# A gated MLP's products computed turned, and a short product placed inside a longer one, in an attention and two-MoE kernel

## The chip, the cores and the metric

The kernel runs on one core of one Trainium2 chip. A core has five engines with a queue each: TensorE (PE, matrix products; PEld is its weight load), VectorE (DVE), ScalarE (ACT), GpSimd (POOL) and SyncE (SP, which issues most DMAs). The metric is the device time of one execution in microseconds (us): the median of three runs of the kernel before is 655.77 us (653.97 to 659.06).

## The reference

Three layers follow one another on 1152 tokens (two sequences of 576) of width 512. In the attention each query keeps its 32 largest scores:

```python
scores = scale * np.matmul(q, k.transpose(0, 1, 3, 2))        # 2 x 8 heads, 576 x 576, head width 64
kth = np.partition(scores, -top_k, axis=-1)[..., -top_k:-top_k + 1]
scores = np.where(scores >= kth, scores, -1000000000.0)
...
x = x / rms * rms_g                                           # first MoE: a gated MLP
g = xn @ w_gate                                               # 512 x 1536
silu = g * (1.0 / (1.0 + np.exp(-g)))
x = silu * (xn @ w_val) @ w_out                               # 1536 x 512
...
expert_idx = np.argmax(x @ w_gate2, axis=1)                   # second MoE: 8 experts, one per token
out[i] = gate_w[i] * (relu(x[i] @ w1[e]) @ w2[e])             # 512 -> 1024 -> 512
```

## The kernel before

**Tiles and stages.** The tokens go in nine tiles t of 128. The attention goes in 36 pairs p of heads, four to a tile: scores (PE, L317; copied by ACT, L319), the search for the 32nd largest value (DVE, L324 to L379), weights (ACT L398 and L404, POOL L399), transposes (PE L422) and products with the values (PE L430). When the four pairs of a tile are done, `norm(t)` makes `xn`, the normed tile with features on the partitions (last step: ACT L470, DVE L471), `moe1(t)` computes the first MoE, and `dispatch(t)` sends the tile's rows into the DRAM buffer `disp`, sorted by expert (POOL L621). Then come the experts of the second MoE, e = 0 to 7, each with an up product, a down product and a send of rows to the output.

**The first MoE (L479 to L536).** Every f32 matrix is kept as a high and a low f16 half, and one product takes three f16 matmuls (high by high, high by low, low by high). A tile has six blocks b of 512 hidden features, a gate block and a value block for each of three groups g. One block is 12 matmuls at L502: a 128x128 piece of `xn` is loaded, 512 columns of weight stream through, and the result `a` has tokens on the partitions. Gate and value are joined elementwise into `h` (L509 to L523). Before the down product, `turned` (L483) transposes `h` with four f32 matmuls (L486) into a PSUM tile, and `halves` (L469) makes `hT` from it on ACT (L470) and DVE (L471). The down product is 36 matmuls a tile (L531). In the last tile, t = 8, `after(...)` fixes which PE instruction follows which.

**What sets the order.** Each stage is a generator. A table of slots says which generator steps when (`at`, L693 to L713), `ahead` gives a step a priority, and a scheduler with a clock of its own places every instruction into its engine's queue from these priorities and from what is free. Each engine then works through its queue in order, and an instruction that waits holds all behind it. So an edit that changes the number and the length of matmuls can move other work in every queue.

**The tail.** While tiles 7 and 8 finish, the first expert weights are loaded as f32 (L779; tiles `raw` and `split`), squared on ACT to find a scale (`size`, L795), and split into f16 halves by ACT (L820) and DVE (L822, L825). `dispatch(7)` and `dispatch(8)` follow the last two tiles: on DVE `scr` (L606) gives each token its place, POOL's L621 scatters the rows. Expert 0's rows come in two parts: `gather("a", ...)` (SP, L836) fetches the 128 rows that tiles 0 to 7 have surely filled ("a"), and `rest_gather` (POOL L903, SP L907) fetches 48 later rows into `xbT` ("b"). `gather(1, ...)` fetches expert 1's rows. On PE the order of the source is `up("a")`, `down("a")`, `up("b")`, `send("a")`, `up(1)`, all products at L920.

## Time and profile before

| quantity | kernel before |
|---|---|
| median of 3 runs | 655.77 us (653.97 to 659.06) |
| profiled execution | 654.35 us, of which span 652.4 us |
| PE busy | 583.8 us (89%), 4817 matmuls |
| PE weight loads busy | 409.2 us (63%) |
| DVE busy | 533.5 us (82%) |
| ACT busy | 501.6 us (77%) |
| POOL busy | 355.6 us (55%) |

The span is the time between the first and the last instruction of the trace; the profiled execution's own time is 1.95 us more. Matmuls overlap, so the busy time of PE is not a sum of work: the distance from one matmul's start to the next one's, which a row with a count gives, is what a matmul takes from the engine. In a row, `x12` counts instructions, and `[2.98 <-DMA xbT<-xb]` says that the engine stood idle for 2.98 us before the row and which event ended that.

### The profile page before, as it was taken

Reading aid. Unit: us, or ns where it says so; the run is one execution under the profiler, and the core shown is the slowest. Engines: PE = TensorE matmul, PEld = TensorE weight load, DVE = VectorE, ACT = ScalarE, POOL = GpSimd, SP = SyncE. Lnnn points to the kernel's source line nnn. Section 1 sums busy time; section 2 is a strip of 40 time slices with the busy share of each in tenths; the row PEclk is TensorE's granted clock in tenths of the full one; section 3 lists DMA queues with packets and bytes.
Section 4 is the critical chain, followed back from the end, with each engine's and each line's share of the span. In section 5 each row is a group of like instructions: output and inputs, shape, how many; then the busy total and the mean of one; then the engine's idle time right before and its main releaser. Section 6 shows DMA issues by size and latency. Waiting matters only on the chain.

```text
span 652.4 us, 13434 instructions
## 1 busy us (share of the span) xinstructions
PE 583.8 (89%) x4817; PEld 409.2 (63%) x4817; DVE 533.5 (82%) x1439; ACT 501.6 (77%) x972; POOL 355.6 (55%) x490
## 2 busy tenths in 40 slices
PE   1427879799999999999999999999999879999995
PEld 1314455445666666767666666565555579999994
DVE  3989999968989979998988999882359756999951
ACT  4469978997787968978887889786499538999811
POOL 2487644646358879958878789686121310123312
PEclk9999979899999999999999999999999989999998
DMA  8998345923000010100000000004900479999201
GB/s 233 296 329 292 118 175 194 311 76 78 30 13 29 14 49 10 34 18 26 18 10 34 16 13 14 2 1 179 354 16 8 156 192 390 340 321 359 97 23 43
DMA packets 47006, 80.05 MB, mean 123 GB/s; under 512 B 18716, under 2 KB 23324, under 8 KB 46930
## 3 DMA queue, kind: packets, MB, share of 16 engines
q1 hardware_dynamic: 45138, 74.28, 35.2%
q0 software_dynamic: 1792, 4.83, 1.9%
q8 instruction: 39, 0.64, 0.4%
q14 instruction: 37, 0.30, 0.1%
HBM read 64.35 MB, written 12.27 MB: 117 GB/s over the span
## 4 chain that ended last, share of the span: by engine, by line
PE 61%; DMA 10%; DVE 9%; ACT 8%; POOL 6%; issue 3%; SPq 2%; POOLq 0%; DVEq 0%; ACTq 0%
PE pm L502 16%; PE acc L920 15%; PE pm L531 9%; PE xps L430 6%; PE tp L317 5%; PE tp L422 4%; ACT junk L795 3%; DMA disp<-wraw 2%; DMA wbig<-in_k_l_dram 2%; DVE r L373 2%; PE pm L486 2%; POOL pp L399 1%; DVE wbig L168 1%; DMA raw<-in_w_dram 1%; DVE wbig L169 1%
## 5 line engine op out<-in xcount | busy, mean ns | idle before, releaser
L502 PE MATMUL pm<-wbig,xn 128*128 128x512 f16 x600 | 145.4, 379 | 0.5 <-DVE hT L471 0.5
L920 PEld LDWEIGHTS <-split 128*128 128x128 f16 x1728 | 114.8, 99 | 5.1 <-DMA xbT<-xb 3.2
L399 POOL TENSOR_TENSOR pp<-s,pp 128x576 f32<-128x576 f32 x72 | 102.1, 1434 | 23.1 <-ACT pp L398 22.9
L502 PEld LDWEIGHTS <-xn 128*128 128x128 f16 x648 | 62.6, 98 | 60.6 <-issue 0.9
L376 DVE MAX8 m<-r 128x8 f32<-128x288 f32 x216 | 96.7, 452 | 2.5
L373 DVE MATCH_REPLACE8 r<-m,r 128x288 f32<-128x288 f32 x216 | 95.2, 443 | 0.0
L317 PE MATMUL tp<-kst,qh 128*128 128x288 f32 (+1 forms) x160 | 64.4, 410 | 32.8 <-ACT s L319 14.9
L531 PE MATMUL pm<-wbig,hT 128*128 128x512 f16 x324 | 76.7, 380 | 0.0
L825 DVE SCALAR_TENSOR_TENSOR split<-raw,sc,split 128x2048 f16<-128x2048 f32 (+1 forms) x32 | 65.9, 2076 | 0.1
L319 ACT ACTIVATE s<-tp 128x288 f32<-128x288 f32 x144 | 57.3, 421 | 10.5 <-PE tp L317 8.8
L423 ACT ACTIVATE pt<-tp 128x384 f32<-128x384 f32 x108 | 52.2, 503 | 15.3 <-PE tp L422 10.8
L317 PEld LDWEIGHTS tp<-kst,qh 128*128 128x128 f32 (+1 forms) x160 | 31.1, 195 | 51.1 <-ACT s L319 21.1
L430 PE MATMUL xps<-pt,vt 128*64 128x128 f32 (+1 forms) x800 | 62.4, 275 | 0.0
L422 PE MATMUL tp<-ident,pp 128*128 128x128 f32 x324 | 57.9, 288 | 4.9 <-DVE r L325 2.6
L398 ACT ACTIVATE pp<-s,bias 128x576 f32<-128x576 f32 x72 | 52.3, 779 | 9.4 <-POOL bias L381 9.3
L920 PE MATMUL acc<-hE,split 128*128 128x168 f16 (+2 forms) x864 | 58.9, 228 | 0.3 <-DVE hE L932 0.3
L404 ACT ACTIVATE pp<-pp,bias 128x576 f32<-128x576 f32 x72 | 57.1, 795 | 2.3 <-POOL pp L399 2.1
L920 PE MATMUL acc<-xgT,split 128*128 128x168 f16 (+1 forms) x768 | 56.4, 234 | 0.4 <-issue 0.4
L795 ACT ACTIVATE junk<-raw 128x2048 bf16<-128x2048 f32 (+1 forms) x32 | 54.1, 1689 | 3.2 <-DMA raw<-in_w_dram 2.9
L422 PEld LDWEIGHTS tp<-ident,pp 128*128 128x128 f32 x324 | 40.2, 145 | 23.7 <-DVE r L325 3.4
L430 PEld LDWEIGHTS xps<-pt,vt 128*64 128x64 f32 x800 | 43.9, 138 | 13.7 <-issue 12.0
L531 PEld LDWEIGHTS <-hT 128*128 128x128 f16 x324 | 29.8, 98 | 32.0 <-issue 1.0
(237 smaller groups left out, 1225.5 us busy)
## 6 DMA issues: line engine op xcount, KB each, us to landing
raw<-in_w_dram SPq DMA_DIRECT2D x28, 1024.0 KB, 9.4
wbig<-in_w_gate_dram SPq DMA_DIRECT2D x6, 1024.0 KB, 7.7
wbig<-in_w_val_dram SPq DMA_DIRECT2D x6, 1024.0 KB, 9.1
wraw<-in_w_out_dram SPq DMA_DIRECT2D x12, 512.0 KB, 5.9
disp<-wraw SPq DMA_DIRECT2D x18, 257.0 KB, 6.4
qraw<-in_q_l_dram SPq DMA_DIRECT2D x72, 64.0 KB, 2.2
wbig<-in_k_l_dram SPq DMA_DIRECT2D x16, 288.0 KB, 4.0
split<-in_w_dram SPq DMA_DIRECT2D x4, 1024.0 KB, 8.3
```

Of the source, the lines that this page charges most:

```text
L317: nc.tensor.matmul(sp[:c1], x[:, i, :c1], kst[b, hp][:, i, c * HALF:(c + 1) * HALF], start=(n == 0), stop=(n == 1))
L319: nc.scalar.activation(s[:, c * HALF:(c + 1) * HALF], sp, AF.Copy)
L373: nc.vector.match_replace(h[i], to[n - 1][:, i], h[i], -3.0e38)
L376: nc.vector.max(to[n][:, i], h[i])
L399: nc.gpsimd.tensor_tensor(w, s[i], w, op=OP.subtract)
L422: nc.tensor.transpose(tp[:, i, :], p2[:, o:o + P], ident)
L430: nc.tensor.matmul(xps[t][rows, hp, c0:c1], v, w, start=(n == 0), stop=(n == 4))
L502: behind[t, "prod", b] = nc.tensor.matmul(a, xn[:, x + c, :], half(i, lo), start=(c == 0 and n == 0), stop=(c == KC - 1 and n == 2))
L531: nc.tensor.matmul(yps, hT[f // KC][:, KC * hi + f % KC, :], half(i, lo), start=(f == 0 and n == 0), stop=(f == NF1 - 1 and n == 2))
L795: nc.scalar.activation(junk, raw[:, g * 2 * BIG // k:(g + 1) * 2 * BIG // k], AF.Square, accum_out=sc[:, 3 + g:4 + g])
L825: nc.vector.scalar_tensor_tensor(lo[:, r], raw[:, r], sc[:, 1:2], hi[:, r], op0=OP.mult, op1=OP.subtract)
L920: nc.tensor.matmul(a, u[:, c, col * P:(col + 1) * P], v[:, c, :a.shape[-1]], start=(c == 0 and n == 0), stop=(c == nk - 1 and n == 2))
```

## The change

In `moe1` operands change places: for each of the four 128-feature pieces j of a block, a 128x128 piece of weight is loaded and the 128 columns of `xn` stream through. A block is 48 matmuls of 128 columns (L499 of the changed kernel) instead of 12 of 512, and its result already has the features on the partitions. The elementwise steps stay as they are. `turned`, its four transposes and its PSUM tile go; `activated` makes the halves of `hT` straight from `h`, so ACT and DVE read SBUF instead of PSUM. In the last tile each block now follows the block before it, and the whole down product follows block 5.

In the expert part `up("b")` (expert 0's late rows, 96 matmuls of 48 columns) is called inside `up(1)`, ahead of its last group, after 72 of its 96 matmuls. `send("a")` and one `ready()` now come behind both.

```diff
--- before.py
+++ after.py
@@ -480,11 +480,8 @@
         hT = [mx.tile([P, 2 * KC, P], F16, name="hT", bufs=3) for _ in range(3)]
         xn = xnT.pop(t)
 
-        def turned(g, h):
-            tp = pm.tile([P, 4, P], F32, name="pm")
-            for i in range(4):
-                behind[t, "turn", g] = nc.tensor.transpose(tp[:, i, :], h[:, i * P:(i + 1) * P], ident)
-            behind[t, "dve"] = halves(hT[g], tp)
+        def activated(g, h):
+            behind[t, "dve"] = halves(hT[g], h.rearrange("p (j w) -> p j w", j=KC))
 
         h = None
         for g in range(3):
@@ -493,18 +490,19 @@
                 gs = mx.tile([P, DM], F32, name="gs")
             for w in range(2):
                 b = 2 * g + w
-                ahead_of = (None, ("prod", 0), None, ("turn", 0), None, ("turn", 1))[b] if t == NT - 1 else None
+                ahead_of = ("prod", b - 1) if t == NT - 1 and b else None
                 a = late[0].tile([P, DM], F32, name="late") if late and b % 3 else pm.tile([P, DM], F32, name="pm")
-                for c in range(KC):
-                    i = KC * b + c
+                for j in range(KC):
                     with after(t, *ahead_of) if ahead_of else nullcontext():
-                        for n, (x, lo) in enumerate(((0, 0), (0, 1), (KC, 0))):
-                            behind[t, "prod", b] = nc.tensor.matmul(
-                                a, xn[:, x + c, :], half(i, lo), start=(c == 0 and n == 0), stop=(c == KC - 1 and n == 2))
-                    if c == 1:
+                        for c in range(KC):
+                            for n, (x, lo) in enumerate(((0, 0), (0, 1), (KC, 0))):
+                                behind[t, "prod", b] = nc.tensor.matmul(
+                                    a[:, j * P:(j + 1) * P], half(KC * b + c, lo)[:, j * P:(j + 1) * P], xn[:, x + c, :],
+                                    start=(c == 0 and n == 0), stop=(c == KC - 1 and n == 2))
+                    if j == 1:
                         yield
-                    if c == 0 and w == 0 and h is not None:
-                        turned(g - 1, h)
+                    if j == 0 and w == 0 and h is not None:
+                        activated(g - 1, h)
                 yield
                 if w == 0 and ew is nc.vector:
                     behind[t, "tanh", g] = nc.scalar.activation(th, a, AF.Tanh, scale=gdec[:, g:g + 1])
@@ -525,8 +523,8 @@
         for f in range(NF1):
             i = final(6, f)
             if f == (2 if t == NT - 1 else 4):
-                turned(2, h)
-            with after(t, *(("prod", 5) if f < 2 else ("turn", 2))) if t == NT - 1 else nullcontext():
+                activated(2, h)
+            with after(t, "prod", 5) if t == NT - 1 else nullcontext():
                 for n, (hi, lo) in enumerate(((0, 0), (0, 1), (1, 0))):
                     nc.tensor.matmul(yps, hT[f // KC][:, KC * hi + f % KC, :], half(i, lo), start=(f == 0 and n == 0), stop=(f == NF1 - 1 and n == 2))
             if f % 2 == 1:
@@ -917,16 +915,20 @@
         wh, wl = (y.rearrange("p (c f) -> p c f", f=width) for y in w)
         for c in of or range(nk):
             for n, (u, v) in enumerate(((wh, x[0]), (wh, x[1]), (wl, x[0]))):
-                nc.tensor.matmul(a, u[:, c, col * P:(col + 1) * P], v[:, c, :a.shape[-1]],
-                                 start=(c == 0 and n == 0), stop=(c == nk - 1 and n == 2))
-
-    def up(k, e, n, early=None):
+                last = nc.tensor.matmul(a, u[:, c, col * P:(col + 1) * P], v[:, c, :a.shape[-1]],
+                                        start=(c == 0 and n == 0), stop=(c == nk - 1 and n == 2))
+        return last
+
+    def up(k, e, n, early=None, between=None):
         hE[k] = [eb.tile([P, NF2, n], F16, name=f"hE{i}", bufs=2 if n <= W else 1) for i in range(2)]
         for lo, hi in groups(NF2, n):
+            if between and hi == NF2:
+                with tc.issue_after(last.ins):
+                    between()
             a = pacc.tile([P, hi - lo, n], F32, name="acc")
             for c in range(lo, hi):
                 with nullcontext() if early is None or c < early else after(NT - 1, "pe"):
-                    product(a[:, c - lo, :], place(2 * e), (xgT[k][:, :KC], xgT[k][:, KC:]), KC, F2, c)
+                    last = product(a[:, c - lo, :], place(2 * e), (xgT[k][:, :KC], xgT[k][:, KC:]), KC, F2, c)
             hh, hl = (x[:, lo:hi, :] for x in hE[k])
             nc.scalar.activation(hh, a, AF.Relu)
             nc.vector.scalar_tensor_tensor(hl, a, 0.0, hh, op0=OP.max, op1=OP.subtract)
@@ -1035,10 +1037,9 @@
         fetch_w()
 
     down("a", 0, WA)
-    up("b", 0, WB)
+    up(1, 1, W, between=lambda: up("b", 0, WB))
     ready()
     send("a", WA, True)
-    up(1, 1, W)
     ready()
     down("b", 0, WB)
     ready()
```

Lines after the edits move by two or three: L502 of before is L499, L531 is L529, L606 is L604, L621 is L619, L795 is L793, L822 and L825 are L820 and L823, L836 is L834, L920 is L918.

The first place is PE's queue around the attention's last value products (`xps<-pt,vt`). Before:

```order
L502 MATMUL pm<-wbig,xn 128x512
L502 LDWEIGHTS xn
L502 MATMUL pm<-wbig,xn 128x512
L430 MATMUL xps<-pt,vt_633 64x128 x10
L531 LDWEIGHTS hT
L531 MATMUL pm<-wbig,hT 128x512
L531 LDWEIGHTS hT
```

After:

```order
L499 MATMUL pm<-xn,wbig 128x128
L499 LDWEIGHTS wbig
L499 MATMUL pm<-xn,wbig 128x128
L430 MATMUL xps<-pt,vt_633 64x128 x10
L529 LDWEIGHTS hT
L529 MATMUL pm<-wbig,hT 128x512
L529 LDWEIGHTS hT
```

What stands behind the last of these value products, up to the first product of expert 0, was 132 products at L502, 84 at L531 and 24 transposes at L486; now it is 576 short products at L499 and 96 at L529, so the value products stand ahead of more of the first MoE.

The second place is DVE's queue at the end of the first MoE: `scr` is the step of `dispatch(7)`, `hT` the last half of tile 8, and `split` are expert weights being split. Before:

```order
L604 TENSOR_SCALAR nm<-nm 128x1
L808 TENSOR_SCALAR sc<-st 128x1
L606 SCALAR_TENSOR_TENSOR scr,pos<-px,oh 128x8
L607 RECIPROCAL nm<-nm 128x1
L809 TENSOR_SCALAR sc<-sc 128x1
L810 TENSOR_SCALAR sc<-sc 128x1
L471 TENSOR_TENSOR hT<-pm,hT 128x512
L825 SCALAR_TENSOR_TENSOR split_5991<-raw_5993,sc,split_5991 128x1024 x2
L822 TENSOR_SCALAR split_5992<-raw_5994,sc 128x1024 x2
L825 SCALAR_TENSOR_TENSOR split_5992<-raw_5994,sc,split_5992 128x1024 x2
L565 TENSOR_SCALAR yn<-yn 128x1
```

After:

```order
L602 TENSOR_SCALAR nm<-nm 128x1
L605 RECIPROCAL nm<-nm 128x1
L471 TENSOR_TENSOR hT<-gs,hT 128x512
L823 SCALAR_TENSOR_TENSOR split_7599<-raw_7601,sc,split_7599 128x1024 x2
L820 TENSOR_SCALAR split_7600<-raw_7602,sc 128x1024 x2
L823 SCALAR_TENSOR_TENSOR split_7600<-raw_7602,sc,split_7600 128x1024 x2
L604 SCALAR_TENSOR_TENSOR scr,pos<-px,oh 128x8
L563 TENSOR_SCALAR yn<-yn 128x1
```

`scr` of tile 7 stood ahead of the last `hT` and of six split instructions; now it stands behind all of them.

The third place is PE's queue in the expert part, where `hE` with `split_5990` (after: `split_7598`) is `down("a")`, `xbT` is `up("b")` and `xgT` with `split_5991` (after: `split_7599`) is `up(1)`. Before, at the end of `up("b")`:

```order
L920 LDWEIGHTS split_5989
L920 MATMUL acc<-xbT,split_5989 128x48
L961 MATMUL back<-ident,yT_6497 128x128 x4
L920 LDWEIGHTS split_5991
L920 MATMUL acc<-xgT,split_5991 128x168
```

After, near the beginning of `down("a")`:

```order
L918 LDWEIGHTS split_7598
L918 MATMUL acc<-hE_8172,split_7598 128x128
L803 LDWEIGHTS ones_70
L803 MATMUL st<-sc,ones_70 128x1
L918 LDWEIGHTS split_7599
L918 MATMUL acc<-xgT,split_7599 128x168
L918 LDWEIGHTS split_7599
```

`up(1)` used to begin behind all of `down("a")` and all of `up("b")`; now 30 of its matmuls stand behind only 12 of the 96 of `down("a")`, the other 84 stand between and behind those 30, then 42 more of `up(1)`, all 96 of `up("b")`, and the last 24 of `up(1)`.

## Rows read from the trace of the kernel before

**Rows 1.** Windows: busy us of each engine (and instructions) in a stretch, PE clock, DMA.
```profile
146.00:180.00 34.00, 34.00 (x206) 20.47 (x205) 30.74 (x92) 25.71 (x56) 18.36 (x24) 1.00 0.22 59
180.00:260.00 80.00, 79.11 (x539) 51.53 (x537) 70.51 (x236) 65.75 (x148) 63.46 (x86) 1.00 0.08 23
515.00:537.00 22.00, 17.48 (x317) 16.89 (x317) 15.46 (x37) 9.48 (x14) 4.16 (x4) 0.92 0.63 164
560.00:600.00 40.00, 40.00 (x551) 39.84 (x549) 39.96 (x51) 39.53 (x44) 8.32 (x5) 1.00 1.09 342
```

**Rows 2.** Groups by line and form: busy us, mean ns of one | idle before.
```profile
L502 PE MATMUL pm<-wbig,xn 128*128 128x512 f16 x600 | 145.4, 379 | 0.5 <-DVE hT L471 0.5
L920 PEld LDWEIGHTS <-split 128*128 128x128 f16 x1728 | 114.8, 99 | 5.1 <-DMA xbT<-xb 3.2 <-issue 1.5
L920 PE MATMUL acc<-xgT,split 128*128 128x128 f16 x96 | 5.7, 219 | 0.0
```

**Rows 3.** Timeline of PE: start us, us, what, count [idle before].
```profile
494.95 0.60 PE L486 MATMUL pm<-ident,gs 128*128 128x128 f32 x4
495.39 2.75 PE L502 MATMUL pm<-wbig,xn 128*128 128x512 f16 x12
...
518.54 4.18 PE L920 MATMUL acc<-xgT,split 128*128 128x128 f16 x72
```

**Rows 4.** Groups by line: halves, and DVE with two SBUF inputs.
```profile
L471 DVE TENSOR_TENSOR hT<-pm,hT 128x512 f16<-128x512 f32 x27 | 18.4, 682 | 14.3 <-ACT hT L470 14.3
...
L452 DVE TENSOR_TENSOR x<-x,rs 128x512 f32<-128x512 f32 x1 | 0.9, 922 | 0.0
L452 DVE TENSOR_TENSOR xu<-xu,rs 128x512 f32<-128x512 f32 x1 | 0.7, 693 | 0.0
```

**Rows 5.** Timeline of PE: the first score product of pair 13.
```profile
199.05 0.48 PE L317 MATMUL tp<-kst,qh 128*128 128x288 f32 x1
```

**Rows 6.** Waits of DVE from 180 to 445 us: us in total, times, longest.
```profile
DVE r L324 <- ACT s L319: 10.9, 16, 3.4
```

**Rows 7.** Timeline of PE: the last value products, and the end of the last down product.
```profile
457.68 1.31 PE L430 MATMUL xps<-pt,vt 128*64 128x128 f32 x20
...
506.95 6.64 PE L531 MATMUL pm<-wbig,hT 128*128 128x512 f16 x30
```

**Rows 8.** Timeline of DVE at the end of the first MoE.
```profile
506.45 0.15 DVE L606 SCALAR_TENSOR_TENSOR scr<-px,oh 128x8 f32<-128x8 f32 x1
...
509.47 0.69 DVE L471 TENSOR_TENSOR hT<-pm,hT 128x512 f16<-128x512 f32 x1 [2.67 <-ACT hT L470]
510.08 2.47 DVE L825 SCALAR_TENSOR_TENSOR split<-raw,sc,split 128x1024 f16<-128x1024 f32 x2
512.47 1.41 DVE L822 TENSOR_SCALAR split<-raw,sc 128x1024 f16<-128x1024 f32 x2
```

**Rows 9.** Timeline of POOL: the scatters of tiles 7 and 8.
```profile
508.71 1.10 POOL L621 DMA_INDIRECT disp<-yd,slot  x1 [0.29 <-POOL slot L619]
...
520.99 1.27 POOL L621 DMA_INDIRECT disp<-yd,slot  x1 [1.57 <-ACT junk L795]
```

**Rows 10.** Timeline of SP: the issue of gather "a".
```profile
511.66 1.36 SPq L836 DMA_TRANSPOSE xgT<-disp  x1
```

**Rows 11.** DMA issues from 500 to 545 us: count, median us from issue to landing.
```profile
xgT<-disp SPq DMA_TRANSPOSE x5, 3.7
disp<-yd,slot POOLq DMA_INDIRECT x2, 3.0
```

**Rows 12.** Timeline of PE in the expert part.
```profile
514.94 1.51 PE L920 MATMUL acc<-xgT,split 128*128 128x128 f16 x24
...
532.06 3.84 PE L920 MATMUL acc<-xbT,split 128*128 128x48 f16 x96 [2.98 <-DMA xbT<-xb]
...
536.21 5.24 PE L920 MATMUL acc<-xgT,split 128*128 128x168 f16 x70
...
543.20 0.52 PE L920 MATMUL acc<-hE,split 128*128 128x48 f16 x14
```

## The prediction

> **What bounds the kernel now.** I read the windows first. From 146 us to the end of the first MoE the reader is to see PE busy nearly all the time (34.00 of 34 us, then 79.11 of 80), while DVE is busy 30.74 of 34 and 70.51 of 80 [rows 1]. So PE is the bound there, but DVE, which searches the top 32, has only 10 to 12 in 100 to spare. Between 515 and 537 us no engine is full: PE works 17.48 of 22 us [rows 1]. There a chain of short steps and transfers sets the time: `dispatch(8)`, its scatter, gathers, and 2.98 us of PE waiting for `xbT` [rows 8 to 10, 12]. From 560 to 600 us PE, DVE and ACT are all full and the DMA share is 1.09 [rows 1], so time lost before that stretch cannot be made good in it.
>
> Second I read the distance between matmul starts, as busy times overlap. Twelve products of 512 columns take 2.75 us, the last of them 0.379 alone, so (2.75 - 0.38) / 11 = 0.2155 us each [rows 2, 3]. Short ones, 128x128 with a new weight each: (4.18 - 0.22) / 71 = 0.0558 [rows 2, 3]. Four transposes of `gs` begin 0.44 us before what follows, 0.11 each [rows 3].
>
> The sum is made against the profiled execution, 654.35 us, which is 1.4 below the median of 655.77.
>
> **The turned products, on PE alone.** They remove 108 transposes (3 groups, 9 tiles, 4 each): 108 x 0.11 = 11.9 us. They replace 648 long products, 139.6 us, by 2592 short ones, 144.6 us: 5.0 more. Net -6.9 us. Here a rule stands against the change. The short rows show 0.0558 us, though each loads its weight anew [rows 3]. The Trainium skill, "TensorE: Matmul & The Clock Gate", section "Back-to-back issue gap", says that a sustained stream of load and matmul pairs runs at about 81 ns each at 128 columns and about 131 ns at 512. By these figures the edit would cost 2592 x 0.081 - 648 x 0.131 = 125 us more instead of 5.0, an estimate from that page. The trace contradicts both figures on this kernel's own rows.
>
> **The halves.** ACT and DVE now read `h` in SBUF; DVE's subtraction took 682 ns from PSUM [rows 4]. The two rows of DVE on 128x512 with both inputs in SBUF take 693 and 922 ns [rows 4]: 0.01 to 0.24 us more for each of 27, of which some 16 lie in the top-k stretch, so 0.2 to 3.8 us of DVE time there. I take the lower end as zero, since 693 is nearest to what stands here, and keep 3.8 for the range.
>
> **Where PE's gain goes.** The order pieces show that the scheduler has used the shorter first MoE to put attention earlier in PE's queue. Behind the last value products stand now 576 x 0.0558 + 96 x 0.2155 = 52.8 us of first-MoE work, before 132 x 0.2155 + 84 x 0.2155 + 24 x 0.11 = 49.2: 3.7 more with rounding. So ahead of them PE has 6.9 + 3.7 = 10.6 us less. Call the end of these products V; before, 457.68 + 1.31 = 458.99 [rows 7]. But attention also needs DVE. At the first score of pair 13, 199.05 us [rows 5], PE's queue held 108 long products, 36 down matmuls and 12 transposes, 32.4 us; now it holds 288 short ones and 24 down matmuls, 21.2. So the order asks for 11.2 us of lead there. What DVE left idle until then is 34 - 30.74 = 3.3 and, at (80 - 70.51) / 80, another 2.3 over 19 us: 5.6 in all [rows 1], and only part of it is waiting for scores (10.9 us of such waits over 180 to 445 us [rows 6]). The rest of the lead PE must stand still for, unless scores and weights wait in buffers: stall S between 0 and 10.6, on these rows 2 to 8. I take 4, as DVE's 5.6 and a buffered microsecond or two cover the rest. V moves by -10.6 + 4 = -6.6.
>
> **The end of the first MoE.** Call E the end of the last down product, before 506.95 + 6.64 = 513.59 [rows 7]. With 3.7 us more behind V, E comes 3.7 later after V; if the last tile's ACT and DVE steps, packed closer, hold PE, up to 5.5.
>
> **`dispatch(7)` gets late.** Before, `scr` of tile 7 ran at 506.45, that is E - 7.1, ahead of the last `hT`, which ended at 510.16 = E - 3.4 [rows 8]. Now it stands behind that `hT` and behind splits of 2.47 + 1.41 + 2.48 = 6.4 us (the second pair like the first), so at E + 3.0; if `hT` comes 2 us earlier, at E + 1. What is queued behind on other engines: POOL's scatter, before 2.26 us after `scr` [rows 8, 9], lands 3.0 later [rows 11], at E + 8.3. Gather "a" waits for it, as it did (issued at 511.66, just when the scatter of 508.71 had landed [rows 9, 10]); with 3.7 us [rows 11] it lands at E + 12.0. Two things wait for that. `up("a")`, which began at 514.94 = E + 1.35 [rows 12], leaves PE idle for about 10 us. And the scatter of tile 8 writes the buffer that gather "a" reads, so it can't start before E + 12.0 and lands at E + 15.0; before it landed at 520.99 + 3.0 = E + 10.4 [rows 9, 11]. That is 4.6 us later after E.
>
> **`up("b")` inside `up(1)`.** Before, from the scatter's landing, 523.99, to the end of `up(1)`, 543.20, it took 19.2 us [rows 9, 12], with the 2.98 us wait for `xbT` in it. Now 30 matmuls of `up(1)` stand ahead of most of `down("a")` and wait for gather 1, which like gather "a" is issued when its scatter has landed, and takes 3.7 us [rows 10, 11]. Behind it follow 96 matmuls of 168 columns at (5.24 - 0.24) / 69 = 0.0725, 84 at 0.0558 and 96 of 48 columns at (3.84 - 0.21) / 95 = 0.038 [rows 12]: 7.0 + 4.7 + 3.7 = 15.4. With 0.1 for the issue that is 19.2. The wait for `xbT` is covered, but `down("a")`, which used to run while the gathers were on their way, now waits with them. So this edit is worth nothing; had `down("a")` kept its place, it would be 3.0. The weight loads and the later experts hang on the same landing, so all behind moves with it.
>
> **The sum.** 654.35 - 6.6 + 3.7 + 4.6 + 0 = 656.05, say 656: no change that can be measured.
>
> **The rivals.**
>
> Faster: PE's whole saving reaches the end. Attention follows PE's order without a stall, `scr` is not what the scatter of tile 8 waits for, and the `xbT` wait is gone: 654.35 - 6.9 - 3.0 = 644.5. For it speaks that PE is full for 370 us; against it the place of `scr` and the waiting `down("a")`, both fixed in the queues.
>
> Slower: DVE paces the attention alone. PE stands still early by the whole 10.6, V stays, and the later tail remains: 654.35 + 3.7 + 4.6 = 662.7. For it speaks DVE's 88 to 90 in 100; against it the 10.9 us in which DVE waited for scores. It decides from S = 8.8 on, where the sum passes 660.9.
>
> Slower by far: weight loads pace the short products. One load alone shows 0.099 us [rows 2]; if loads did not overlap with matmuls, 2592 x (0.099 - 0.056) = 111 us would be added, about 765. Against it stand 72 in sequence at 0.0558, a load with each [rows 3]. The issue gap on the skill's page named above points the same way.
>
> The change doesn't do what it says: if ACT, not PE, paced the tiles, neither the saving nor the earlier V would appear; then the tail's +8.3 alone is the slower rival again.
>
> **How the numbers follow.** About 1% (6.5 us) is what a measurement of this kernel can tell from no change. The forecast, with S from 0 to 8, `scr` 2 us earlier or not, E up to 1.8 later and the halves' 3.8, spans 650 to 662 in its likely part: 0.59. The faster rival has 0.18, the slower one 0.21, the weight loads 0.02. Faster by over 1%: 0.18; within: 0.59; slower: 0.23. The range reaches from 647, between forecast and faster rival, to 664, past the slower one.
>
> **What the profile would show.** Turns: no L486, short products 0.056 apart. Attention: PE waits for DVE or ACT of about 4 us in all between 150 and 210 us, and the last value products end near 452. Tail: `scr` of tile 7 some 3 us after the last down product, and about 10 us of idle PE ahead of `up("a")`. Expert part: no wait for `xbT`, a wait for gather 1 in its place. I am wrong if attention stalls far more or not at all, if the splits on DVE run before the last `hT` is needed, or if short products beside f32 work are farther apart than 0.056.

## The result, and the profile after

The changed kernel takes 663.16 us (median of 8 runs, 660.59 to 664.01) against 654.77 us (8 runs) of the kernel before beside it: a ratio of 1.0103, interval 1.0081 to 1.0125 (the quotient of the two medians is 1.0128, a little outside it). It is slower, by about 1%: inside the range of 647 to 664, at its upper end, and 7 us above the forecast of 656. Its profiled execution took 663.43 us, its span is 661.6.

I read the profile after by cutting the span at five points that both traces have: the start of pair 4's first score product (PE L317), V (end of the last value products), E (end of the last down product), the issue of scatter 8 on POOL, and the end. All times in the tables below are starts or ends of rows in the timelines of the profiled executions.

| stretch, us | before | after | difference | forecast |
|---|---|---|---|---|
| start to pair 4 | 75.64 | 78.92 | +3.3 | 0 |
| pair 4 to V | 383.35 | 372.54 | -10.8 | -6.6 |
| V to E | 54.60 | 63.43 | +8.8 | +3.7 |
| E to issue of scatter 8 | 7.40 | 10.39 | +3.0 | +4.6 |
| scatter 8 to the end | 131.44 | 136.27 | +4.8 | 0 |
| span | 652.43 | 661.55 | +9.1 | +1.7 |

The first line is not the change. Among the profiles of all kernels here, which run the same code up to that point, pair 4 begins between 75.6 and 80.7 us in the five with the old first MoE and between 76.9 and 78.9 in the nine with the turned one. The kernel before and the one of e9 are the two ends (timelines of PE, start us, us, what):

```profile
75.64 0.38 PE L317 MATMUL tp<-kst,qh 128*128 128x288 f32 x1
```
```profile
80.73 0.38 PE L317 MATMUL tp<-kst,qh 128*128 128x288 f32 x1
```

So the profile of before happens to start early, and the other four lines, +5.8 us in all, are the change; the interval of the ratio says 5 to 8. Each stretch was read from one execution of each kernel.

**The page and the windows after.** First the busy times of the engines (page), then the windows that answer [rows 1]:

```profile
PE 580.1 (88%) x6653; PEld 477.1 (72%) x6653; DVE 529.6 (80%) x1439; ACT 502.3 (76%) x972; POOL 360.0 (54%) x490
```
```profile
146.00:180.00 34.00, 33.59 (x403) 27.99 (x401) 33.16 (x107) 28.87 (x65) 22.35 (x28) 1.00 0.26 69
180.00:260.00 80.00, 79.28 (x952) 66.84 (x952) 76.88 (x258) 69.10 (x157) 65.05 (x83) 1.00 0.09 26
515.00:537.00 22.00, 14.61 (x178) 14.03 (x179) 12.17 (x35) 9.92 (x14) 4.37 (x8) 0.77 0.47 101
560.00:600.00 40.00, 39.09 (x539) 38.79 (x537) 39.26 (x44) 39.55 (x43) 8.49 (x5) 1.00 1.09 319
```

In the top-k stretch PE is as full as before, and DVE has gone from 30.74 and 70.51 us [rows 1] to 33.16 and 76.88: more of DVE's work is done in the same time. Between 515 and 537 us PE works 2.9 us less (17.48 before) and its granted clock fell from 0.92 to 0.77. From 560 to 600 us PE, which was full, now has 0.9 us of gaps.

**Attention and products.** Groups by form, waits of PE from 146 to 260 us, and PE's timeline (answers to [rows 2, 3, 7]):

```profile
L499 PE MATMUL pm<-xn,wbig 128*128 128x128 f16 x2400 | 168.0, 221 | 2.8 <-DVE th L509 0.9 <-ACT gs L520 0.8 <-DVE xn L471 0.7
```
```profile
PE pm L529 <- DVE hT L471: 0.7, 1, 0.7
PE pm L238 <- ACT wbig L241: 0.4, 1, 0.4
```
```profile
450.15 1.31 PE L430 MATMUL xps<-pt,vt 128*64 128x128 f32 x20
...
466.91 3.29 PE L499 MATMUL pm<-xn,wbig 128*128 128x128 f16 x56
...
485.33 4.29 PE L499 MATMUL pm<-xn,wbig 128*128 128x128 f16 x46 [0.45 <-DVE xn L471]
...
512.13 2.75 PE L529 MATMUL pm<-wbig,hT 128*128 128x512 f16 x12
```

The short products run (3.29 - 0.22) / 55 = 0.0558 us apart, as the 128-column rows of before said. PE waits for DVE or ACT only 1.1 us in the 114 us where I had looked for a stall of 4. V is at 451.46, E at 514.88.

How far ahead attention came by pair 13 is shown by PE's first score of that pair (timeline; before in [rows 5]) and by two windows, the kernel before first. They begin 70.36 us behind the start of pair 4 in each and end at DVE's first step of pair 13 (L324, at 201.38 and 190.99):

```profile
187.89 0.40 PE L317 MATMUL tp<-kst,qh 128*128 128x288 f32 x1
```
```profile
146.00:201.38 55.38, 55.38 (x358) 34.65 (x356) 49.02 (x153) 42.53 (x95) 32.36 (x45) 1.00 0.15 42
149.28:190.99 41.71, 41.68 (x509) 35.17 (x508) 40.89 (x134) 34.98 (x82) 25.48 (x33) 1.00 0.19 53
```

Counted from pair 4 this score comes 14.4 us earlier (108.97, before 123.41), and DVE's first step of the pair 13.7. DVE's idle time in the window fell from 6.4 to 0.8 us, and its busy time from 49.02 to 40.89: 8.1 us of its other steps now stand behind that step.

**From V to scatter 8.** ACT's last step for `xn` of tile 8 (in the kernel before it began at 478.36), the windows of PE behind it, and the timelines of DVE and POOL (answers to [rows 8, 9]):

```profile
483.98 0.58 ACT L470 ACTIVATE xn<-xps 128x512 f16<-128x512 f32 x1
```
```profile
483.00:490.00 7.00, 5.28 (x60) 5.02 (x61) 6.19 (x11) 7.00 (x10) 0.00 (x0) 0.76 0.00 0
```
```profile
508.55 0.69 DVE L471 TENSOR_TENSOR hT<-gs,hT 128x512 f16<-128x512 f32 x1
509.16 2.48 DVE L823 SCALAR_TENSOR_TENSOR split<-raw,sc,split 128x1024 f16<-128x1024 f32 x2
511.55 2.31 DVE L820 TENSOR_SCALAR split<-raw,sc 128x1024 f16<-128x1024 f32 x2
513.78 2.47 DVE L823 SCALAR_TENSOR_TENSOR split<-raw,sc,split 128x1024 f16<-128x1024 f32 x2
516.17 0.15 DVE L604 SCALAR_TENSOR_TENSOR scr<-px,oh 128x8 f32<-128x8 f32 x1
```
```profile
509.39 2.30 POOL L608 TENSOR_SCALAR yd<-nm,yn 128x1 f32<-128x1 f32 x1
...
517.49 1.12 POOL L619 DMA_INDIRECT disp<-yd,slot  x1 [0.33 <-POOL slot L617]
...
525.28 1.06 POOL L619 DMA_INDIRECT disp<-yd,slot  x1 [4.42 <-DMA notes<-disp]
```

`xn` of tile 8 ends 33.1 us after V; before it was 20.0 (478.94 - 458.99). PE runs dry, and its first 46 products behind the gap are (4.29 - 0.22) / 45 = 0.0904 us apart instead of 0.0558 while the granted clock of the window is 0.76: another 1.6 us. Then `scr(7)` stands behind `hT` and three pairs of splits, as read from the queues. Scatter 8 waits 4.42 us for a fetch from `disp` (`notes`, which SP issues right behind gather "a").

**Experts.** PE's timeline from gather "a" on (answers to [rows 12]), the window with the granted clock behind gather "a", and DVE's timeline at the first of three places where PE later waits for it:

```profile
523.78 8.28 PE L918 MATMUL acc<-xgT,split 128*128 128x128 f16 x96 [1.63 <-DMA xgT<-disp]
...
533.57 0.60 PE L918 MATMUL acc<-xgT,split 128*128 128x168 f16 x6 [0.84 <-DMA xgT<-disp]
...
543.48 2.59 PE L918 MATMUL acc<-xbT,split 128*128 128x48 f16 x96
...
594.33 2.42 PE L918 MATMUL acc<-hE,split 128*128 128x168 f16 x31 [0.91 <-DVE hE L934]
610.39 2.55 PE L918 MATMUL acc<-hE,split 128*128 128x168 f16 x33 [0.97 <-DVE hE L934]
623.22 6.99 PE L918 MATMUL acc<-hE,split 128*128 128x168 f16 x94 [1.27 <-DVE hE L934]
```
```profile
523.00:529.00 6.00, 5.22 (x50) 5.21 (x50) 1.39 (x2) 1.45 (x2) 1.58 (x2) 0.50 0.15 49
```
```profile
591.33 2.34 DVE L823 SCALAR_TENSOR_TENSOR split<-raw,sc,split 128x2048 f16<-128x2048 f32 x1
593.59 1.09 DVE L934 SCALAR_TENSOR_TENSOR hE<-acc,hE 128x504 f16<-128x504 f32 x2
```

`up("a")` begins 8.9 us after E and half of it runs at 1.2 GHz (granted clock 0.50); `xbT` is no longer waited for, gather 1 is, 0.84 us. `up("b")` follows at once. In the later experts two `hE` steps stand together behind weight splits of 2.34 us, and PE waits 0.91 + 0.97 + 1.27 = 3.2 us for them. In the kernel before PE had no wait for `hE` in the later experts.

### The profile page after: what moved, and what is told of

Its sections match the earlier page's. It is cut to its first block, busy times and chain, and to the rows that moved or that the text cites. A ratio compares the mean times of both kernels' runs of the same rounds, so it can differ in the third digit from the quotient of the medians.

```text
span 661.6 us, 17083 instructions
## 1 busy us (share of the span) xinstructions
PE 580.1 (88%) x6653; PEld 477.1 (72%) x6653; DVE 529.6 (80%) x1439; ACT 502.3 (76%) x972; POOL 360.0 (54%) x490
## 4 chain that ended last, share of the span: by engine, by line
PE 30%; DVE 24%; DMA 14%; POOL 12%; ACT 9%; issue 8%; SPq 3%; POOLq 0%; DVEq 0%; ACTq 0%
PE pm L499 9%; PE acc L918 7%; DVE split L823 4%; DMA vt<-in_v_l_dram 4%; PE pm L529 4%; DVE r L373 4%; PE xps L430 3%; DVE m L376 3%; PE tp L317 3%; POOL pp L399 2%; ACT junk L793 2%; PE tp L422 2%; DMA wbig<-in_w_val_dram 2%; DMA raw<-in_w_dram 2%; DMA disp<-yd,slot 2%
## 5 line engine op out<-in xcount | busy, mean ns | idle before, releaser
L499 PE MATMUL pm<-xn,wbig 128*128 128x128 f16 x2400 | 168.0, 221 | 2.8 <-DVE th L509 0.9
L499 PEld LDWEIGHTS <-wbig 128*128 128x128 f16 x2592 | 156.6, 99 | 17.4 <-issue 6.3
L918 PEld LDWEIGHTS <-split 128*128 128x128 f16 x1728 | 116.0, 99 | 10.1 <-issue 7.2
L399 POOL TENSOR_TENSOR pp<-s,pp 128x576 f32<-128x576 f32 x72 | 102.9, 1445 | 19.0 <-ACT pp L398 18.5
L376 DVE MAX8 m<-r 128x8 f32<-128x288 f32 x216 | 95.1, 450 | 1.6
L317 PE MATMUL tp<-kst,qh 128*128 128x288 f32 (+1 forms) x160 | 63.2, 400 | 32.4 <-ACT s L319 15.0
L529 PE MATMUL pm<-wbig,hT 128*128 128x512 f16 x324 | 78.2, 380 | 1.8 <-ACT hT L470 0.9
L823 DVE SCALAR_TENSOR_TENSOR split<-raw,sc,split 128x2048 f16<-128x2048 f32 (+1 forms) x32 | 65.9, 2078 | 0.3 <-ACT split L818 0.3
L317 PEld LDWEIGHTS tp<-kst,qh 128*128 128x128 f32 (+1 forms) x160 | 31.6, 197 | 47.0 <-ACT s L319 21.8
L918 PE MATMUL acc<-xgT,split 128*128 128x168 f16 (+1 forms) x768 | 59.0, 241 | 3.6 <-DMA xgT<-disp 2.5
L918 PE MATMUL acc<-hE,split 128*128 128x168 f16 (+2 forms) x864 | 59.4, 229 | 3.2 <-DVE hE L934 3.2
L423 ACT ACTIVATE pt<-tp 128x384 f32<-128x384 f32 x108 | 49.7, 496 | 12.2 <-PE xps L430 6.9
L430 PE MATMUL xps<-pt,vt 128*64 128x128 f32 (+1 forms) x800 | 57.9, 274 | 0.0
L793 ACT ACTIVATE junk<-raw 128x2048 bf16<-128x2048 f32 (+1 forms) x32 | 54.1, 1691 | 1.8 <-DMA raw<-in_w_dram 1.4
L529 PEld LDWEIGHTS <-hT 128*128 128x128 f16 x324 | 29.3, 98 | 31.5 <-DVE hT L471 1.5
L317 PE MATMUL tp<-kst,ql 128*128 128x288 f32 (+1 forms) x160 | 48.7, 310 | 0.0
```

The source lines that it names most:

```text
L317: nc.tensor.matmul(sp[:c1], x[:, i, :c1], kst[b, hp][:, i, c * HALF:(c + 1) * HALF], start=(n == 0), stop=(n == 1))
L376: nc.vector.max(to[n][:, i], h[i])
L399: nc.gpsimd.tensor_tensor(w, s[i], w, op=OP.subtract)
L430: nc.tensor.matmul(xps[t][rows, hp, c0:c1], v, w, start=(n == 0), stop=(n == 4))
L499: behind[t, "prod", b] = nc.tensor.matmul(a[:, j * P:(j + 1) * P], half(KC * b + c, lo)[:, j * P:(j + 1) * P], xn[:, x + c, :], start=(c = ...
L529: nc.tensor.matmul(yps, hT[f // KC][:, KC * hi + f % KC, :], half(i, lo), start=(f == 0 and n == 0), stop=(f == NF1 - 1 and n == 2))
```

## The experiments

Each edit is made to the changed kernel unless it is said otherwise. "Before" is the kernel before on the same chip beside it: 655.91 us for e1 to e4, 656.45 for e5 to e8, 655.48 for e9 to e12. The stretches of all profiles, us:

| kernel | median | ratio to before | pair 4 to V | V to E | E to scatter 8 | scatter 8 to end |
|---|---|---|---|---|---|---|
| before | | | 383.35 | 54.60 | 7.40 | 131.44 |
| after | 663.16 | 1.0103 (1.0081 to 1.0125) | 372.54 | 63.43 | 10.39 | 136.27 |
| e1 turned alone | 662.01 | 1.0111 (1.0074 to 1.0149) | 372.56 | 62.94 | 10.28 | 134.19 |
| e2 up b alone | 659.05 | 1.0053 (1.0028 to 1.0077) | 382.97 | 54.59 | 7.31 | 135.41 |
| e3 xn ahead of squares | 662.84 | 1.0137 (1.0086 to 1.0189) | 372.58 | 60.35 | 14.77 | 134.99 |
| e4 scr ahead of splits | 659.57 | 1.0070 (1.0039 to 1.0102) | 372.55 | 61.79 | 11.52 | 133.88 |
| e5 tile 7's products first | 670.09 | 1.0212 (1.0195 to 1.0229) | 372.49 | 58.74 | 10.71 | 148.26 |
| e6 scatter chain freed | 658.28 | 1.0025 (1.0008 to 1.0042) | 372.54 | 58.75 | 11.03 | 136.75 |
| e7 e2, weight's sums behind | 663.18 | 1.0114 (1.0089 to 1.0140) | 383.17 | 54.60 | 7.32 | 138.48 |
| e8 all freed | 660.65 | 1.0072 (1.0053 to 1.0091) | 372.55 | 58.54 | 11.06 | 137.89 |
| e9 before, fewer splits | 655.29 | 0.9993 (0.9973 to 1.0012) | 382.92 | 54.60 | 7.48 | 132.54 |
| e10 e2, fewer splits | 659.11 | 1.0055 (1.0033 to 1.0078) | 382.84 | 54.61 | 7.49 | 134.56 |
| e11 after, fewer splits | 658.60 | 1.0053 (1.0028 to 1.0079) | 372.53 | 61.41 | 12.00 | 132.98 |
| e12 slot ahead of splits | 656.83 | 1.0028 (1.0002 to 1.0054) | 372.00 | 58.76 | 10.06 | 135.35 |

### e1: the turned products alone

```diff
-    up(1, 1, W, between=lambda: up("b", 0, WB))
+    up("b", 0, WB)
     ready()
     send("a", WA, True)
+    up(1, 1, W)
```

> The turned products alone; the expert part keeps its old order (up b and the send ahead of up 1). In the trace of the changed kernel the last value products end at 451.5 us against 459.0 before, but the end of the first MoE comes 8.8 us later behind them, tile 8's scatter 3.0 later behind that, and the experts behind up 1 take 4.7 more. Theory T (the tail of the first MoE): the loss is the order that the turned products leave in the queues of ACT and DVE at the end of the first MoE; up b's new place has no part in the first two losses. This kernel then keeps 7.5 of gain and 8.8 + 3.0 of loss, waits for xbT again, and gets back the 4.7 only if they belong to up b's place: 658 to 663 us, slower than before. Rival B (the new place of up b is what costs): 645 to 651 us, faster than before.

Measured 662.01 us. By the ratios the turned products alone carry the whole loss, and with the late rows' edit on top nothing is won. The stretches show the gain of 10.8 us up to V, 8.3 and 2.9 lost from V to scatter 8, 2.8 behind it. They add up to +3.2, less than the medians' 6.1; the profiled execution (659.38 us) is the fastest of the four.

### e2: the late rows inside expert 1's first product, alone

The kernel before with only the expert part of the diff.

> Up b inside up 1 alone; the first MoE is computed as before. In its queue down a stays whole and ahead of up 1, which it does not in the changed kernel. Theory T: the 2.98 us wait for xbT is covered and nothing else moves ahead of it, 650.5 to 653.5 us, if the experts behind do not lose; the 4.7 us that the later experts lose in the changed kernel would show here too if they come from this edit, 655 to 658. Rival B: 658 or more.

Measured 659.05 us, 3.1 above before. Up to scatter 8 nothing differs. From there to the end of `up(1)` and `up("b")` it takes 19.0 us, before 22.4: the wait for `xbT` is covered, 3.4 us won. But `up(2)` starts 28.7 us behind scatter 8, before 25.0. ACT's and PE's timelines of this kernel show what came between:

```profile
541.45 1.91 ACT L795 ACTIVATE junk<-raw 128x2048 bf16<-128x2048 f32 x1 [5.23 <-DMA raw<-in_w_dram]
```
```profile
543.50 0.16 PE L805 MATMUL st<-sc,ones 128*128 128x1 bf16 x1 [1.13 <-ACT junk L795]
...
547.32 0.16 PE L805 MATMUL st<-sc,ones 128*128 128x1 bf16 x1 [3.13 <-ACT junk L795]
```

PE's sums of a weight's squares (L805) stand ahead of `down("b")`, their squares on ACT wait for the weight's load, and `hE` of the late rows stands behind those squares. PE's wait for one transfer has become a wait for another.

### e3: xn of tile 8 ahead of the weights' squares

```diff
     with after(NT - 1, "sq"):
         size(0, 0)
+    with after(NT - 1, "xn"), after(NT - 1, "xn high"):
         size(1, 1)
-    with after(NT - 1, "xn"), after(NT - 1, "xn high"):
         convert(0, 0)
-    size(2, 2)
+        size(2, 2)
```

> The changed kernel, but the squares of the second and third weight matrix may only be placed behind the step on ACT that finishes xn of the last tile; six of the nine squares that stood ahead of it now stand behind it. Theory T: xn of tile 8 comes up to 6 x 1.18 = 7.1 us earlier, the last down product 5 to 7, and the step scr of tile 7 now stands behind one pair of splits instead of three, so tile 8's scatter gains 3 or more on top: 652 to 657 us. A rival that has the loss in the 146 us at the start (3.0 us later there) or in up b's place: 660 to 664, as the changed kernel.

Measured 662.84 us, no gain. V to E became 3.1 us shorter, but `xn` of tile 8 still ended 31.4 us after V, and ACT's timeline names what held it:

```profile
481.07 0.60 ACT L470 ACTIVATE xn<-xps 128x512 f16<-128x512 f32 x1 [5.57 <-PE pm L499]
```

The squares had held `xn` only for the last 1.7 us. What holds it here is PE's own products: `xn` has one buffer, and the last products that read tile 7's stand on PE behind some 24 down matmuls. E to scatter 8 grew by 4.4, since PE now had 21 products of `up("a")`, waiting for gather "a", ahead of tile 8's token counts.

### e4: scr(7) ahead of DVE's last splits

```diff
-    with after(NT - 1, "dve"):
+    with after(NT - 1, "dve"), after(NT - 2, "scr"):
         convert(2, 2, False, (2, 3))
...
-    with after(NT - 1, "dve"), after(NT - 1, "tanh", 2):
+    with after(NT - 1, "dve"), after(NT - 1, "tanh", 2), after(NT - 2, "scr"):
         convert(3, 3, True, (0, 1))
```

A third line, left out here, enters `scr` in the table `behind` that `after(...)` reads.

> The changed kernel, but the last splits on DVE may only be placed behind the step scr of tile 7; in the queue that this gives, down a also stays whole ahead of up 1. Nothing is done for xn of tile 8. Theory T: scr runs when PE's count for tile 7 is there, at about 512.3 instead of 516.2, so tile 8's scatter and all behind it come up to 4 us earlier, and down a no longer waits with up 1: 656 to 660 us. If scr's place costs nothing: 661 to 664.

Measured 659.57 us, 3.6 below the changed kernel. Counted from E, `scr(7)` ran 3.8 us earlier (at 508.73, E is 511.23), scatter 7 only 0.8, for this reason (timelines of DVE and POOL):

```profile
508.82 2.47 DVE L823 SCALAR_TENSOR_TENSOR split<-raw,sc,split 128x1024 f16<-128x1024 f32 x2
```
```profile
509.05 1.16 POOL L607 TENSOR_SCALAR pos<-pos 128x1 f32<-128x1 f32 x1
510.31 2.40 POOL L617 TENSOR_SCALAR slot<-pos 128x1 int32<-128x1 f32 x1
...
513.00 1.81 POOL L619 DMA_INDIRECT disp<-yd,slot  x1 [0.29 <-POOL slot L617]
```

POOL's operations on one element per partition, 0.24 and 0.38 us when DVE is not splitting, take 1.16 and 2.40 beside the splits. E to scatter 8 did not fall (11.5); the gain against the changed kernel lies in V to E (1.6) and behind scatter 8 (2.4).

### e5: tile 7's products ahead of its down product

```diff
-            with after(t, "prod", 5) if t == NT - 1 else nullcontext():
+            with after(t, "prod", 5) if t >= NT - 2 else nullcontext():
```

> The changed kernel with one thing added: token tile 7's last products (f-loop after product 5) are bound to stand behind all of that tile's gate and value products, as tile 8's already are, so that PE does not put 20 or more products of the last MoE step ahead of the last products that read xn of tile 7. Theory X (the one buffer of xn is held until tile 7's last product is issued, and so tile 8's norm, its products and everything behind come late): xn of tile 8 ends 28 to 30 us behind the last value product instead of 33.1, the last down product of tile 8 comes 58 to 60 us behind the last value product instead of 63.4, and the time falls to 658 to 661. Rival (the loss in this stretch is ACT's and DVE's load there, not the buffer): xn stays at 31 to 33, the stretch at 62 to 64, the time at 662 to 664.

In its stretch theory X held: `xn` of tile 8 ended 26.6 us after V instead of 33.1, even before the 28 to 30 expected, and V to E was 58.7 (timeline of ACT; V is 449.68).

```profile
475.74 0.58 ACT L470 ACTIVATE xn<-xps 128x512 f16<-128x512 f32 x1
```

The time forecast for it missed by 10 us. Counted from pair 4, scatter 8 came 4.4 us earlier than in the changed kernel, but behind it the experts lost 12, in code that the edit doesn't touch (timelines of ACT and PE):

```profile
559.80 1.91 ACT L793 ACTIVATE junk<-raw 128x2048 bf16<-128x2048 f32 x1 [5.00 <-DMA raw<-in_w_dram]
```
```profile
566.73 3.10 PE L918 MATMUL acc<-hE,split 128*128 128x168 f16 x21 [4.53 <-DVE hE L934]
```

The scheduler had drawn the queues anew: squares that wait 5.00 us for a weight's load stood ahead of `hE` on ACT, and PE waited 4.53 for it, the longest of several new waits. Expert 2 took 27.5 us (`up(2)` to `up(3)`), before 15.0.

### e6: e5, scr as in e4, and tile 7's small steps on DVE

```diff
-        ev = nc.vector if t == NT - 1 else nc.gpsimd
+        ev = nc.vector if t >= NT - 2 else nc.gpsimd
```

> The changed kernel with three things: the one of e5, scr(7) ahead of DVE's last weight splits as in e4, and the small operations of tile 7's dispatch on DVE instead of POOL (as tile 8's are). Theory X with theory Y (the way to the two scatters is lengthened by DVE's splits: scr behind them, and POOL's small operations stretched beside them): last value product to last down product 58 to 60 us, scatter 8 at 6 to 8 us behind the last down product (10.4 in the changed kernel, 11.5 in e4), time 653 to 657, so the kernel before's time. If only Y holds: stretch 62 to 64, scatter 8 at 6 to 8, time 657 to 660. If only X holds: scatter 8 stays at 10 or more, time 657 to 660.

Measured 658.28 us. X again gave 58.7. Y did not show: E to scatter 8 stayed at 11.0, the case "only X holds". DVE's and POOL's timelines say why:

```profile
505.69 0.15 DVE L604 SCALAR_TENSOR_TENSOR scr<-px,oh 128x8 f32<-128x8 f32 x1
...
505.77 2.47 DVE L823 SCALAR_TENSOR_TENSOR split<-raw,sc,split 128x1024 f16<-128x1024 f32 x2
...
511.94 0.26 DVE L617 TENSOR_SCALAR slot<-pos 128x1 int32<-128x1 f32 x1
```

```profile
520.49 1.06 POOL L619 DMA_INDIRECT disp<-yd,slot  x1 [4.31 <-DVE yd L572]
```

The splits that had stood ahead of `scr` now stood between `scr` and the slot numbers. And scatter 8 itself waited last for tile 8's rows `yd` (DVE L572, at 518.96), which stood behind one more pair of splits; in e4 it was the same step (5.38 us).

### e7: e2 with one weight's sums behind the late rows

```diff
-    ready()
     send("a", WA, True)
+    down("b", 0, WB)
+    ready()
     ready()
-    down("b", 0, WB)
     ready()
...
-            size(ORDER[n + 1], n + 1)
+            with after("b", "hE") if n == 4 else nullcontext():
+                size(ORDER[n + 1], n + 1)
```

The diff is against e2; a third line, left out here, enters `hE` in the table `behind`.

> The kernel of e2 (expert 0's late rows inside expert 1's first product, nothing else changed from the kernel before), with the squares and sums of one later weight (the half of expert 2's second load) put behind the late rows' relu and behind their second product. Theory Z (in e2 PE gained 3.4 us by hiding the transposed load of the late rows, and lost it and more since PE's sum of squares stood ahead of the late rows' second product and waited for that weight's load): PE has no wait at a sum of squares ahead of expert 2's first product, which starts 21 to 24 us behind scatter 8 (28.7 in e2, 25.0 before), and the time is 652 to 656. Rival (the weights' loads set expert 2's start in any case, the wait only moves on): expert 2's products start or stop for the weights again, its start plus the waits in it is 27 to 29 us behind scatter 8, time 657 to 661.

Both halves of the expectation happened, one after the other. `up(2)` started 21.4 us behind scatter 8, as Z says. Then expert 2 took 22.2 us instead of 15.0, and the time was 663.18, worse than e2 and than the rival's 657 to 661 (timeline of PE):

```profile
555.09 0.16 PE L805 MATMUL st<-sc,ones 128*128 128x1 bf16 x1 [2.48 <-DVE split L825]
...
557.00 4.77 PE L920 MATMUL acc<-hE,split 128*128 128x168 f16 x44 [1.74 <-DVE hE L936]
```

### e8: e6 with e7's edit

> The kernel of e6 with e7's edit: both parts of the change, tile 7's products first, the scatter chain freed, the weight's sums behind the late rows' second product. If X, Y and Z hold: 647 to 652, below the kernel before. If Z falls: as e6, 653 to 657. If X or Y falls: 651 to 656.

Measured 660.65 us: a miss by 9 us for the hoped case, above all three cases, and 2.4 worse than e6. Scatter 8 to the end took 137.9. Moving the sums didn't help here either.

### e9, e10, e11: fewer splits in the experts' stage

```diff
-        for g in low[:k]:
+        for g in low[:k] if n < 5 else ():
```

The low halves of the weights from the sixth load on aren't computed; PE multiplies with stale ones, as many as before. e9 is this edit in the kernel before, e10 in e2, e11 in the changed kernel.

> The kernel before, with the low halves of the weights from the sixth load on left out (22 splits of 2.34 us that DVE does in the experts' stage; PE multiplies with what stood there before, so as many products run). It is the measure for the next two. Theory W (in the experts' stage DVE's splits are as full as PE, so that whatever PE gains ahead of it comes back as waits for hE behind splits): the kernel before has no PE wait there, so little changes: 651 to 657. If it falls by more, DVE was the bound of that stage in the kernel before too, beyond PE.

> The kernel of e2 (expert 0's late rows inside expert 1's first product alone) with the same 22 splits left out. Theory W: its 3.4 us come through, 2 to 5 us below e9, where e2 was 3.1 above the kernel before. Theory Z2 (not DVE but the weights' loads behind scatter 8, with the squares on ACT, set when expert 2 starts): 0 to 4 us above e9, with PE's waits at sums of squares as in e2.

> The changed kernel with the same 22 splits left out. Theory W: of its 8 us over the kernel before the 4.9 lost behind scatter 8 are gone, the rest (8.8 between the last value product and the last down product, 3.0 on the way to scatter 8, less 7.9 won before) stays: 2 to 5 us above e9, and behind scatter 8 no longer than e9. Rival (the 4.9 are not DVE's): 6 to 9 us above e9.

e9: 655.29 us, as before (0.9993): DVE's splits, though they fill DVE, cost the kernel before nothing that these runs can show (interval of the ratio 0.9973 to 1.0012).

e11: 658.60 us, 3.3 above e9, as theory W says. From 560 to 600 us PE is full again with DVE at 17 of 40 us, and PE's wait for `hE` in the later experts, 3.2 us in the changed kernel, is nearly gone (window of e11, waits of PE from 560 to 640 us):

```profile
560.00:600.00 40.00, 40.00 (x554) 39.90 (x552) 17.43 (x37) 38.03 (x41) 5.39 (x5) 1.00 1.08 356
```
```profile
PE acc L918 <- DVE hE L934: 0.3, 1, 0.3
```

Scatter 8 to the end takes 132.98, in e9 132.54. So DVE's splits ahead of `hE` are shown as the cause of 3.3 of the 4.8 us that the changed kernel loses behind scatter 8 (136.27 to 132.98, as much as the waits that went). The other 1.5 stay open; e9, which has no such waits to lose, also takes 1.1 more there than the kernel before.

e10: 659.11 us, 3.8 above e9. Here W falls: without the splits the late rows' edit costs as much as with them, and PE's wait is where it was in e2 (timeline of PE):

```profile
547.18 0.16 PE L805 MATMUL st<-sc,ones 128*128 128x1 bf16 x1 [3.35 <-ACT junk L795]
```

By these rows e2 loses to the wait for the weight's load; when that is moved (e7), the next shortage in line takes its place.

### e12: e6 with the splits behind tile 7's slot numbers

```diff
-    with after(NT - 1, "dve"), after(NT - 2, "scr"):
+    with after(NT - 1, "dve"), after(NT - 2, "slot"):
         convert(2, 2, False, (2, 3))
...
-    with after(NT - 1, "dve"), after(NT - 1, "tanh", 2), after(NT - 2, "scr"):
+    with after(NT - 1, "dve"), after(NT - 1, "tanh", 2), after(NT - 2, "slot"):
         convert(3, 3, True, (0, 1))
```

> The kernel of e6 with DVE's last splits placed behind tile 7's slot numbers instead of only behind scr(7): in e6 scr(7) ran at 505.7 but the 6.2 us of splits stood between it and the slot numbers at 511.9, and scatter 7 was issued at 513.0. Theory Y: scatter 7 at 506 to 509, scatter 8 at 6 to 8 us behind the last down product (11.0 in e6), time 3 to 4 us below e6, 653 to 656, just below the kernel before. Rival (tile 8's own chain sets scatter 8 and the splits only move into it): scatter 8 still 10 to 11 behind, 657 to 659.

Measured 656.83 us, the best of the turned kernels, at 1.0028 (1.0002 to 1.0054) not below before. Scatter 7 came at 506.16, as theory Y says. Scatter 8 did not follow, 10.06 us behind E: there the rival held (timelines of POOL, PE and DVE):

```profile
506.16 1.36 POOL L619 DMA_INDIRECT disp<-yd,slot  x1 [1.92 <-DVE slot L617]
...
518.53 1.26 POOL L619 DMA_INDIRECT disp<-yd,slot  x1 [1.24 <-DVE slot L617]
```
```profile
514.20 2.72 PE L918 MATMUL acc<-xgT,split 128*128 128x128 f16 x24 [1.80 <-DMA xgT<-disp]
```
```profile
516.99 0.17 DVE L604 SCALAR_TENSOR_TENSOR scr<-px,oh 128x8 f32<-128x8 f32 x1 [2.54 <-PE px L597]
```

24 products of `up("a")`, which wait 1.80 us for gather "a", stand on PE ahead of tile 8's counts, and `scr(8)` waits 2.54 us for those. In the kernel before `up("a")` did not wait for this gather; here, with E 4.7 us earlier after V, it does. Putting the counts ahead of these products wasn't tried.

## Why the prediction was right or wrong

**The time.** The range held it, but not the likeliest case's sum: the ratio of 1.0103 lies on the border between "within 1%" and slower. Against the +1.7 of the sum the four stretches give +5.8; their errors are -4.2, +5.1, -1.6 and +4.8, and the signs partly cancel. The other 3 us of the miss lie ahead of pair 4, where the execution that the sum was made against was early; the edits have no part in them.

**Turned products on PE: right in mechanism, the match in part luck.** The pitch is 0.0558, L486 is gone, and V came 10.8 us earlier where PE was to have 10.6 less. But from pair 4 to V PE's idle time rose by 2.4 us (13.8 to 16.2, windows of the two stretches), so its work there fell by 13.2, 2.6 more than in the sum; where these come from stays open. The rival of slow weight loads falls. By the Trainium skill's figures ("TensorE: Matmul & The Clock Gate", "Back-to-back issue gap") the products alone would have cost 125 us more, an estimate; this run contradicts them: of 2393 distances between neighbours among its 2592 short products 2295 are 0.053 to 0.057 us.

**The stall S: mis-sized, 4 forecast, 2.4 measured.** That is the rise of PE's idle time from pair 4 to V; of it only 0.7 lies in the 114 us from 146.00 on (from 149.28 in the changed kernel). The lead that the order asked for, 11.2 us, was there at pair 13, and more (14.4). The 5.6 us of idle time were read rightly, and they were used up (5.5). The step that failed is "a buffered microsecond or two cover the rest": I took DVE's work ahead of pair 13 as fixed, but the new order puts 8.1 us of it behind that pair.

**The halves: a price is there, without effect.** DVE's subtraction took 802 ns on average over 26 of the 27, before 682: 3.1 us in all, of the 0.2 to 3.8 put down for the range. The median is 684, so the lower end fits most of them, and three long ones carry much of the rest. PE waited 0.7 us for them up to 260 us.

**The slower rival: its number, not its mechanism.** 662.7 is nearly the time measured, but DVE did not pace the attention: V came 10.8 us earlier, where that rival leaves it in place.

**V to E: mis-sized, +3.7 (up to 5.5) forecast, +8.8 measured.** The count of matmuls behind V was right: with the one further cause taken away (e5, e6, e12) +4.1 is left. The other 4.7 I did not see: the single buffer of `xn`, held by tile 7's last products, and behind it the squares on ACT and the fallen clock. e3, which moves only the squares, wins 3.1 in this stretch; e5, which frees the buffer, wins all 4.7, and with it only five of the ten squares stand ahead of `xn`. The order showed both queues; I summed matmuls and did not ask which of them frees a buffer.

**The way to scatter 8: right in mechanism, 3.0 instead of 4.6.** `scr(7)` ran at E + 1.3, the case "`hT` comes 2 us earlier", and scatter 8 waited for the fetch of "a" from `disp`. PE's idle time ahead of `up("a")`, 8.9 us from E, was foreseen as about 10.

**`up("b")` inside `up(1)`: right, and for the stated reason.** From scatter 8 to the block's end 22.6 us, before 22.4: the `xbT` wait is gone, one for gather 1 has come. The sum's 0.038 us for a product of 48 columns was read from a row at the lower clock, though: behind the `xbT` wait the granted clock was 0.54, near the lower level (532.06 to 535.74), and at 1.00 in the changed kernel it is (2.59 - 0.22) / 95 = 0.025, 1.2 us less for the 96. But that it would be worth 3.0 had `down("a")` kept its place is wrong: e2 is that kernel, and the 3.4 us it gains are lost again to the weights' load behind it (e2, e10).

**"All behind moves with it": wrong, +4.8.** I read from [rows 1] that PE, DVE and ACT are all full from 560 to 600 us, concluded that no time can be made good there, and did not ask the other way round, whether a new order could lose some. With DVE full, three `hE` steps behind splits became PE waits of 3.2 us; e11 takes the splits away, and 3.3 of the loss goes.

**Open.** Why every variant with all splits needs 2.4 to 17 us more behind scatter 8 than the kernel before is shown for most of the changed kernel's loss (e11) and read from the rows of e2 and e5, for e2 with e10 against the splits as the cause; for the others it is only likely to be the same. Whether tile 8's counts ahead of `up("a")` would bring scatter 8 forward (e12) wasn't tried. What moves the start of pair 4 by up to 5 us between profiles wasn't looked into.

## What to carry to other kernels

Behind a saved microsecond ask what was tuned to the old arrival: here 10.8 us won in attention were paid back at a single-buffered tile, in a scatter chain and in a stage where a second engine is full. When a scheduler places the queues, an edit in one stage draws all later queues anew, so a change is compared stretch by stretch from common marks, and a stretch without an edit counts too. A full engine beside the bound is no proof that it costs something, nor that it doesn't: leaving its work out, as in e9 and e11, tells.

## What the runs showed of the hardware

POOL operations on one element per partition took 0.24 to 0.38 us alone and 1.16 to 2.40 us while DVE ran splits whose operands all lie in SBUF; DVE's plain splits (L820) were stretched too, a pair from 1.41 us to 2.31 in the changed kernel. The Trainium skill, "SBUF — State Buffer", section "SBUF: two separate sides", says that DVE and GpSimd share a pair of ports, which one instruction locks for its whole length, among others a DVE operation with two SBUF inputs against a GpSimd one that reads SBUF. The trace agrees with it: in the changed kernel POOL's step of 2.30 us ends at 511.69, the pair of splits (L823) beside it at 511.64.

The turned products brought DVE under this too. `hT` before was made from PSUM, and all 27 subtractions took 671 to 693 ns; from SBUF three of them took 1.11, 1.86 and 1.92 us, each beside a product of POOL's (L399) of 1.4 us or more.

Behind 8.9 us in which PE was busy for 2.23 us its granted clock was 0.50 (1.2 GHz) from 523 to 529 us. The 96 products of 128 columns there came (8.28 - 0.22) / 95 = 0.085 us apart on average instead of 0.0558, 2.8 us more in all, so this late start cost more than its wait.
